# The last 800 steps of a hand-ordered attention and MLP kernel in another order, some copies and masks on another engine

## The chip, the cores and the metric

The kernel runs on one NeuronCore of a Trainium2 chip. It has five engines that each work through their own list of instructions in order: TensorE (PE; its weight loads are shown as PEld), VectorE (DVE), ScalarE (ACT), GpSimd (POOL) and SyncE (SP, here only an issuer of DMAs). The metric is the device time of one execution in microseconds: 209.23 us, the median of three runs (209.04 to 209.62).

## The reference

Windowed attention with four sink keys, then an MLP with a squared relu, on four batches of 768 tokens with eight heads of 64:

```python
scores = scale * np.matmul(q, k.transpose(0, 1, 3, 2))
keep = is_sink | in_window          # key < 4, or 0 <= query - key < 128
a = softmax(np.where(keep, scores, -1e9))
x = np.matmul(a, v)                 # heads side by side: 3072 x 512
h = x @ w_in                        # 512 x 2048
r = np.maximum(h, 0.0)
out = (r * r) @ w_out               # 2048 x 512
```

## The kernel before

Each batch is six blocks of 128 tokens, taken as three pairs s = 0, 1, 2. For a batch, queries and keys are brought to a transposed layout `qkT`: batches 0 and 1 by TensorE (`transpose`, L503, then `unload` through L192 or L194), batches 2 and 3 by DMA transpositions that SP issues (`turn`, L460) from bf16 copies `qn`, which POOL's DMAs load (L402). For each pair and two head pairs, TensorE makes scores (`ps`, L609), ScalarE exponentials (`expm`, L630), and the window's triangles are masked, on DVE (L642 or, for a batch's first pair, L639) or on POOL in two instructions (L218). TensorE multiplies by the values (`po`, L678), DVE normalizes (L694, L695) into `xn_sb`. That is transposed to `xT`, by TensorE (L727) or, in batches 2 and 3, by SP (L709).

Layer 1 (L762, L892) works in PSUM tiles `pm`. From batch 1 on it uses a scheme with seven products in place of eight: sums `wi` of weights and `xs` of tokens stand as operands, copies of partial results `t` (L192 on ACT, L194 on DVE) are added by a custom DVE instruction (L942) or go through a relu (L967, L969), and the result is squared into `gT_sb` (L915 on ACT, L917 on DVE). For one pair of blocks alone the tokens are first spread by a copy `xd<-xT` on ACT (L192). Layer 2 (L1239) does the same per pair of blocks, called tile (b, u): four sums of `gT_sb` on DVE (L1213, into `sg` or in place), seven products into `py`, evacuations to `osb` (L192, L194, L1253), and a store by SP (L1282, 512 KB). The very last tile (3, 2) has a form of its own (L1058, L1100, L1125, L1141, L1148) whose stores are four of 128 KB (L1168, L1183, L1186).

Nothing plans at run time or build time. The 992 steps are created in a fixed order and numbered by it; a table of words, `ORDER`, says in which order they are issued. A word is the step's number, a letter for the engine (d, a, g; none where the step has its first choice), and after a + the PSUM pool of a tile, 0 or 1 for the first or second of the pools that it may take. `Plan.run` (L94) walks the table: it takes a room for each tile that a step needs, first free first, issues the step, and gives rooms back after their last reader. So the table sets each engine's order, and with it which earlier reader a new tile waits for.

```python
for word in words:
    word, *chosen = word.split("+")
    n = int(word.rstrip("pdag"))
    o = self.ops[n]
    o.engine = names[word[-1]] if word[-1] in names else next(iter(o.engines))
    for s in o.takes:
        if len(s.pools) > 1:
            s.pool = s.pools[int(chosen.pop(0))]
        s.room = free[s.pool].pop(0)
    o.run(o.engine)
```

PSUM has two pools, `att` and `den`, of two rooms each; a room holds one tile of two banks. The SBUF pool `qr` of five rooms holds the `qn` tiles, so that batch 3's loads wait for batch 2's turns.

Of the kernel before, what the change touches and what calls it, by code (L numbers as in the profile page):

```python
# [22 lines left out]
63a 68+0 75+1 88d 69 70 76+1 22 71+0 77 23 72 73 78 24 94a 79+1 90+0 93d 92a 95+1 80 91d 81 96a 74 100+0 82 101+0 25  # L23
26 102 83+1 97d 66 84d 27 104 85 110+1 111+0 103g 86d 152+1 112 28 113d 105d 98+0 99 153 106+0 108 114 115d 154a 116+1
118 29 160+1 109 161 162a 107 30 119 117 120+0 31 155d 163a 122 121d 123d 32 168+0 156+1 331 33 172+0 157 169 164+1
170a 165 34 35 158d 173 166a 124+1 125a 127+0 36 159d 176+1 129a 177 126d 174a 140+1 133+1 37 128d 171d 142 136 180+1
181 282+0 38 178d 167d 137d 132+0 141+1 182a 130+0 39 283 40 144 143d 41 134 42 43 332 284 285 131 145d 146+0 175a 147
135g 278 179a 286 138+1 139 287 288 148+0 150 334 151d 44 149a 279 183d 289 184+1 290 185 193+0 280 281 200+0 201 291
194 45 204+1 196+0 202 46 203 205 198a 186 197 207a 293 206 187+0 199a 216+0+0 47 48 195a 217 49 188d 234+1+0 50 235
190+0 219 208+0 87 292 237 209 295 191 218 297+0 189 220 51 336 52 212 53 210a 294 211 255+0 252+1 254 299 298 256 54  # L30
253a 257 444 223+0+1 333 238d 445 192a 226 304 213 224 221+0 312 222 300 241+1+0 301 214+0 296 244 215 302 225 446
303d 242 306 260+0+0 236 462 263 307 314 337 316+0 245d 243d 315 227 308 313 447 318 319 464 246+0 261 247 239+0 448
240 320 321 228+0 475 322d 317 229 258+0 335 259 325 449 450 310 326 230+0 451 231 452 232 248+0 233 249a 327 250 251a
323 309 305 343+1 359+1 339 338 344 467 340 345 341 360 463 329 311 453 324 328 346 465 347 361 362 363 267+1+1 348
349 350 364 268 342 365d 270 351d 366 367 375+0 352 376 377 354 368 454 355 468 356d 370 369a 357 455 391+0 456 379
264 457 262 466 458 265+0 271 393 353 459 378 269 371 392 395 358a 266 372 272+0 373 381 380 382 474 374a 397 394 273
274+0 383d 276 277 396 275a 384 469 407 386 485+0+0 388d 718 472 387 470 460 486 398 410 461 408 389 412+1 488 471
478+1+0 409 399 473 385 479 400 487 330 413 688 402 414 428+0 404 401 403 405 430 416 429 418 432 406a 489 530+0 481
415 390 417 431 419 532 689 526 411 490+0 434 420 433 435 528 421 423 491 436 437 707 482 527 422a 533 424 480 534 690
708 476+0 477 425 439 440 441 691 535 442 531 483+1 426 529 484 443a 536 494+0+0 537 438a 497 692 427 495 568+0 545  # L40
539 540 570 564 566 492 693 694 695 542 498d 501+0+0 502 565 696 541 493 571 504 697 706 538 572 698 543 569 709
517+0+1 518 546 699 573 544 547 520 700 575 503d 510+0+0 701 574 549+0 496d 583 711 576 567 577 584 578 521d 513 505
579 585 551 581 506+0 552 580 507 514 511 586 512d 553 519 713 588+0 499+0 710 500 554 702 703 555d 515+0 516 522+0
589 719 550 590 712 523 591 745+0+0 748 592 558 556 548 560 746 738+0+0 741 594d 557 593 587 595 559 562 739 561
722+0+0 747 596d 714 604+0 749d 725 597 606 599 605 600 726 601 608 607 715 508 509 723 602 524 716 525 717 656+1 657
598 720+0 658 609 620 721 659 610 622 640+0 750+0 724 611 642 612 621 641 751 613 742 603a 660 662 740 615 644 623 646
614 727+0 616 704 661 617 663 563 643 645 618 647 619 672+0 664 667 665 648 651 649 728 582 674 668 673 669 650 676
670 743+0 652 666a 675 744 653 624+1 678 671a 677 654 626 679 625 729+1+0 680 730 628 770 681 655 630 683 774+0 771
732 684 627 775 685 686 629 772 776 754+0+1 682a 755 731 631 777 687 733 773 632 734+0 735 778 635 779 757 705 761+1+0
633 637 636 781 752 758 780d 634 762 638 756 639a 736 793+0 783 789 764 790 784 759+0 737 791 785 795 760 763 782 765  # L50
794 827 828 800 832+1 766+0 786 787 767 848+0 788 850d 829 833 808 796 834 835 830 849 797 768 836 838d 810 851 753
798 837 852 812+1 792 839 853 799 854 855 856 769 801 802 804 840d 859 803 841 857 831 814 843 815 858 842a 866 844
861 805d 816 845 811 809 806 860 817 868+0 813 862 864 846 819 865 818 863 869 870 884+1 867 871 821 872 885 874 823
886d 873 875 822 847 876 916+0 824 887 888 917 889 932 825 877 878 879 890 934 820 918 880 919 920 900+1 807 902 881d
882 933 891 921 883a 901 892 904 936+0 922d 938 906 903 923 905 893 924d 895 896 907 925 894a 897 939 935 908d 927 898
928 926a 940 929 937 826 911 909 899a 913 910 930 941 931 912 942 914 943 946 915 970 955+1 944 945 957 951 974+0 948
953 971 947 952 958 975 949 959d 956 972 960 950 961 973 977+0 962 976 978 964 954 966 979d 965 963 980 968 981 982
985 967d 969 983 984 989 986 988 987
"""
DUMMIES = {  # L60
    57: 9, 62: 14, 95: 7, 83: 3, 991: 29,
# [1348 lines left out]
```

## Time and profile before

| what | us |
|---|---|
| median of three runs | 209.23 |
| profiled execution, its own time | 209.26 |
| its span, first to last instruction | 207.6 |
| busy: PE, PEld, DVE, ACT, POOL | 199.6, 176.2, 174.7, 133.9, 96.2 |
| first changed steps, about | 44 |
| last matmul ends, about | 204.2 |
| last store issued | 204.57 |

A time in the profile is counted from the span's start. Times and lines of the profile are of the kernel before; in the changed kernel every line of the functions has a number higher by four, since the table has four rows more (L218 is L222 there, L1213 is L1217). A busy TensorE may still be waiting a little, since the end of each matmul is modelled and overlaps the start of the next; the idle time of the weight loads shows shorter waits. "issue" as a releaser means that the profile shows nothing that was waited for.

### The profile page before, as it was taken

Reading aid. Unit: us, or ns where it says so; the run is one execution under the profiler, and the core shown is the slowest. Engines: PE = TensorE matmul, PEld = TensorE weight load, DVE = VectorE, ACT = ScalarE, POOL = GpSimd, SP = SyncE. Lnnn points to the kernel's source line nnn. Section 1 sums busy time; section 2 is a strip of 40 time slices with the busy share of each in tenths; the row PEclk is TensorE's granted clock in tenths of the full one; section 3 lists DMA queues with packets and bytes.
Section 4 is the critical chain, followed back from the end, with each engine's and each line's share of the span. In section 5 each row is a group of like instructions: output and inputs, shape, how many; then the busy total and the mean of one; then the engine's idle time right before and its main releaser. Section 6 shows DMA issues by size and latency. Waiting matters only on the chain.

```text
span 207.6 us, 6021 instructions
## 1 busy us (share of the span) xinstructions
PE 199.6 (96%) x2500; PEld 176.2 (85%) x2502; DVE 174.7 (84%) x342; ACT 133.9 (64%) x208; POOL 96.2 (46%) x137
## 2 busy tenths in 40 slices
PE   7969999999899999999999999999999999999993
PEld 7458997579878899889878988998889999999893
DVE  4387657498899998999998778999989998998853
ACT  2769458729998168898888458989871452584010
POOL 7799275699499927999333529000280000000000
PEclk9999999999999999999999999999999999999999
DMA  5999999999999999999999996901023220200205
GB/s 157 220 218 200 186 185 212 180 156 175 159 75 126 147 129 225 117 182 155 123 142 235 103 135 194 115 3 25 12 42 129 53 94 10 104 0 0 104 0 202
DMA packets 96042, 26.10 MB, mean 126 GB/s; under 512 B 86800, under 2 KB 93456, under 8 KB 96016
## 3 DMA queue, kind: packets, MB, share of 16 engines
q0 software_dynamic: 69248, 12.59, 86.5%
q1 hardware_dynamic: 25568, 12.49, 27.2%
q10 hardware_dynamic: 1200, 0.66, 1.1%
q8 instruction: 19, 0.31, 0.6%
q14 instruction: 7, 0.06, 0.1%
HBM read 27.30 MB, written 6.29 MB: 162 GB/s over the span
## 4 chain that ended last, share of the span: by engine, by line
PE 80%; DVE 6%; ACT 6%; DMA 4%; issue 2%; POOL 0%; ACTq 0%; POOLq 0%; DVEq 0%
PE py L1239 28%; PE pm L892 25%; PE pm L762 9%; PE po L678 6%; PE ps L609 4%; DMA v<-in_v_dram 4%; PE py L990 3%; ACT expm L630 2%; PE py L1100 2%; PE pt L503 1%; DVE r L942 1%; ACT gT_sb L915 1%; PE px L727 1%; DVE xn_sb L695 1%; ACT qkT L192 1%
## 5 line engine op out<-in xcount | busy, mean ns | idle before, releaser
L630 ACT ACTIVATE expm<-ps 128x1024 bf16<-128x1024 f32 (+1 forms) x48 | 43.8, 951 | 9.6 <-PE ps L609 7.6
L218 POOL TENSOR_SCALAR_AFFINE_SELECT expm<-expm 128x512 bf16<-128x512 bf16 x34 | 24.0, 740 | 42.2 <-DVE xn_sb L695 19.5
L942 DVE CUSTOM_DVE_ANT_0 r<-pm,t 128x512 bf16<-128x512 f32 x54 | 36.0, 684 | 1.6 <-PE pm L892 1.2
L1239 PEld LDWEIGHTS <-gT_sb 128*128 128x128 bf16 x320 | 30.4, 98 | 4.4 <-issue 0.6
L892 PEld LDWEIGHTS <-w_in_sb 128*128 128x128 bf16 x384 | 32.4, 114 | 1.7 <-issue 1.5
L192 ACT ACTIVATE t<-pm 128x512 f32<-128x512 f32 x42 | 24.7, 600 | 13.4 <-PE pm L892 12.7
L892 PEld LDWEIGHTS <-wi 128*128 128x128 bf16 x288 | 24.7, 114 | 0.8 <-issue 0.7
L1239 PEld LDWEIGHTS <-sg 128*128 128x128 bf16 x240 | 22.5, 98 | 3.1 <-DVE sg L1213 0.3
L192 ACT ACTIVATE osb<-py 128x256 f32<-128x256 f32 (+1 forms) x36 | 14.1, 397 | 15.7 <-PE py L1239 15.0
L762 PE MATMUL pm<-xT,w_in_sb 128*128 128x256 bf16 x192 | 22.5, 273 | 0.1
L892 PE MATMUL pm<-xs,wi 128*128 128x256 bf16 (+1 forms) x192 | 21.6, 246 | 0.0
L892 PE MATMUL pm<-xs,w_in_sb 128*128 128x256 bf16 (+1 forms) x192 | 21.5, 246 | 0.0
L762 PEld LDWEIGHTS <-w_in_sb 128*128 128x128 bf16 x192 | 20.5, 114 | 0.8 <-issue 0.5
L1239 PE MATMUL py<-wt,gT_sb 128*128 128x256 bf16 x160 | 20.7, 273 | 0.2
L1239 PE MATMUL py<-wt,sg 128*128 128x256 bf16 x160 | 20.8, 273 | 0.0
L1239 PE MATMUL py<-w_out_sb,gT_sb 128*128 128x256 bf16 x160 | 20.4, 273 | 0.0
L915 ACT ACTIVATE gT_sb<-r 128x1024 bf16<-128x1024 bf16 x17 | 18.0, 1056 | 1.8 <-DVE r L942 1.6
L678 PE MATMUL po<-v,expm 128*128 128x65 bf16 x352 | 17.9, 193 | 1.1 <-DMA v<-in_v_dram 1.1
L678 PEld LDWEIGHTS <-expm 128*128 128x128 bf16 x352 | 16.8, 97 | 2.3 <-issue 1.3
L695 DVE TENSOR_TENSOR xn_sb<-po,rc 128x512 bf16<-128x512 f32 (+1 forms) x28 | 17.2, 615 | 1.0
L1253 DVE TENSOR_TENSOR osb<-py,osb 128x256 f32<-128x256 f32 x30 | 12.1, 416 | 4.7 <-PE py L1239 4.6
L609 PE MATMUL ps<-qkT 64*128 64x128 bf16 (+1 forms) x256 | 14.5, 238 | 1.1 <-ACT expm L630 0.6
(107 smaller groups left out, 377.8 us busy)
## 6 DMA issues: line engine op xcount, KB each, us to landing
out_dram<-osb SPq DMA_DIRECT2D x11, 512.0 KB, 3.0
v<-in_v_dram POOLq DMA_DIRECT2D x24, 128.0 KB, 7.0
qn<-in_k_dram POOLq DMA_DIRECT2D x20, 128.0 KB, 6.6
qn<-in_q_dram POOLq DMA_DIRECT2D x20, 128.0 KB, 6.3
w_in_sb<-in_moe_w_in_dram POOLq DMA_DIRECT2D x4, 512.0 KB, 9.2
w_out_sb<-in_moe_w_out_dram POOLq DMA_DIRECT2D x4, 512.0 KB, 10.5
qr<-in_k_dram SPq DMA_DIRECT2D x4, 256.0 KB, 6.9
qr<-in_q_dram ACTq DMA_DIRECT2D x2, 256.0 KB, 4.2
```

The costliest lines, as they stand in the source:

```text
L192: return nc.scalar.activation(out=dst, in_=src, func=AF.Copy)
L218: nc.gpsimd.affine_select(out=e_tile, in_=e_tile, compare_op=ALU.is_ge, fill=fill, base=i - 1, pattern=[[0, n], [1 if i else -1, 128]], ch ...
L609: nc.tensor.matmul(ps[:, h2, o:o + w], lhsT=qkT_sb[r, m, 1, c, :], rhs=qkT_sb[r, m, 0, qb:qb + w // 128, :], start=(i == 0 and not biased) ...
L630: nc.scalar.activation(out=x[:, :, o:512], in_=bank_t["s", b, s, m][:, :, o:512], func=AF.Exp, scale=scale)
L678: touch(("po", b, s, m0), e, nc.tensor.matmul(pv[:, i, h2, :], lhsT=lhsT, rhs=rhs, start=(n_ == 0), stop=(n_ == len(mms) - 1)), j)
L695: touch(("po", b, s, m0), e, nc.vector.tensor_tensor(out=xn_sb[:, 2 * s:2 * s + 2, 128 * (m0 + j0):128 * (m0 + j0 + nj)].rearrange("p i (j ...
L762: nc.tensor.matmul(pm[:, i, :], lhsT=w_in_sb[:, fb // 4, kb, fb % 4:512:4], rhs=xT[:, c0 // 256:(c0 + cw) // 256, kb, :], start=(kb == 0), ...
L892: touch(tag, e, nc.tensor.matmul(y[:, bk, i, :], lhsT=weights(name, f0 + i, a), rhs=rhs[:, a, :], start=fresh and i == 0 and a == 0, stop= ...
L915: nc.scalar.activation(out=d, in_=x, func=AF.Square)
L942: touch(tag, e, nc.vector._custom_dve(TENSOR_ADD_SAT, out=d.rearrange("p n c -> p (n c)"), in0=T["y"][:, 1].rearrange("p n c -> p (n c)"), ...
L1239: touch((b, u), e, nc.tensor.matmul(region(name), lhsT=x[:, i, :], rhs=w_[:, i, :], start=first and i == 0, stop=i == HB - 1, skip_group_c ...
L1253: ins = nc.vector.tensor_tensor(out=d, in0=region(of), in1=d, op=ALU.add)
```

## The change

Only the table changes. Its first 188 words issue the same steps as before (they carry more letters). From the 189th on, near 44 us, where batch 1's first scores are prepared, the remaining 800 or so steps stand in another order up to the end. Of these, 75 name another engine: on balance four masks more go to POOL (six go there, two come back), and copies, relus and squares are exchanged between DVE and ACT in both directions. Twenty PSUM tiles or so take the other pool. The steps themselves, their matmuls, their sizes and all DMAs are the same.

```diff
 ORDER = """
-990 1 0 2 7 8 9 10 11 12 13 14 15 16 17 18 56d 60a 55d 991+0 3 19 57+0 61d 20 5 6 4 62+1 65 59a 67+0 58a 21 64d 89d
...
-985 967d 969 983 984 989 986 988 987
+990d 1d 0d 2d 7 8a 9 10a 11 12 13 14 15 16 17 18 56d 60a 55d 991+0 3g 19g 57+0 61d 20g 5g 6g 4g 62+1 65g 59a 67+0 58a
...
+965 963d 982 968d 967a 985 969 983d 984d 989 986d 988 987d
 """
```

Three places show how rows move. The first is TensorE at batch 1's first scores (`ps` are scores, `pt` transposes of queries and keys from `qn`). Before, the second score step follows the first directly:

```order
L609 LDWEIGHTS qkT_180
L609 MATMUL ps<-qkT_180 128x256
L609 LDWEIGHTS qkT_180
L609 MATMUL ps<-qkT_180 128x128
L609 LDWEIGHTS qkT_180
L609 MATMUL ps<-qkT_180 128x128
```

In the changed kernel eight transposes, each with its weight load, stand between the first step and the second (one of the eight pairs is shown):

```order
L613 LDWEIGHTS qkT_180
L613 MATMUL ps<-qkT_180 128x128
L507 LDWEIGHTS qn
L507 MATMUL pt<-ident,qn 128x128
...
L613 LDWEIGHTS qkT_180
L613 MATMUL ps<-qkT_180 128x128
```

They are the transposes of the batch's third head pair, which stood ahead of the score steps before.

The second place is SP's queue in batches 2 and 3 (`qkT_179` and `qkT_180` are the layouts of batch 2 and batch 3, `xT_184` is batch 2's token layout). Before:

```order
L1282 DMA out_dram<-osb 128x1024
L460 DMA_TRANSPOSE qkT_179<-qn 128x4x128 x8
L460 DMA_TRANSPOSE qkT_180<-qn 128x4x128 x2
L709 DMA_TRANSPOSE xT_184<-xn_sb 128x4x128 x2
L460 DMA_TRANSPOSE qkT_180<-qn 128x4x128 x2
L1282 DMA out_dram<-osb 128x2x512
L460 DMA_TRANSPOSE qkT_180<-qn 128x4x128 x6
L709 DMA_TRANSPOSE xT_184<-xn_sb 128x4x128 x3
```

Now:

```order
L464 DMA_TRANSPOSE qkT_179<-qn 128x4x128 x7
L1286 DMA out_dram<-osb 128x1024
L464 DMA_TRANSPOSE qkT_179<-qn 128x4x128 x4
L464 DMA_TRANSPOSE qkT_180<-qn 128x4x128 x4
L713 DMA_TRANSPOSE xT_184<-xn_sb 128x4x128 x2
L464 DMA_TRANSPOSE qkT_180<-qn 128x4x128 x6
```

Four turns of batch 3, not two, stand ahead of the first two transpositions of `xT_184`.

The third place is DVE at the sums of layer 2's last two tiles (L1213 is tile (3,1), L1058 tile (3,2); `sg` holds sums). Before:

```order
L1058 TENSOR_TENSOR sg<-gT_sb 128x1024
L1253 TENSOR_TENSOR osb<-py,osb 128x256 x2
L1213 TENSOR_TENSOR sg<-gT_sb 128x1024
L1213 TENSOR_TENSOR sg<-sg,gT_sb 128x1024
L1058 TENSOR_TENSOR gT_sb<-gT_sb 128x8x128
L1213 TENSOR_TENSOR gT_sb<-gT_sb 128x8x128
```

Now:

```order
L1257 TENSOR_TENSOR osb<-py,osb 128x256
L1062 TENSOR_TENSOR sg<-gT_sb 128x1024
L1217 TENSOR_TENSOR sg<-gT_sb 128x1024
L1217 TENSOR_TENSOR gT_sb<-gT_sb 128x8x128
L1217 TENSOR_TENSOR sg<-sg,gT_sb 128x1024
```

One of the two evacuations ahead of the sums went to a later place, and tile (3,1)'s sum in place now precedes its second sum into `sg`.

More of the change, by code (lines that the diff above doesn't have):

```diff
@@ new lines @@
+153 106+0 108 114a 115d 154a 116+1 118 29g 160+1 109d 161 162a 107d 30g 119d 117d 120+0 31g 155d 163a 122 121d 123d
+32g 168+0 156+1 331d 33g 172+0 157 169 164+1 170a 165 34g 35g 158d 173 166a 124+1 125a 127+0 36g 159d 176+1 129a 177
+126d 174a 140+1 133+1 37g 128d 171d 142a 136a 180+1 181 282+0 38g 178d 167d 137d 132+0 141+1 182a 130+0 39g 283 40g
+144a 143d 41g 134a 42g 43g 332d 284 285 131a 145d 146+0 175a 147d 135g 278d 179a 286 138+1 139d 287 288 148+0 150 334d
+151d 44g 149a 279d 183d 289 280d 200+0 196+1 87g 333d 290a 184+1 293d 202a 45g 46g 198d 295d 291a 193+0 185a 194a 201
@@ new lines @@
+203d 47g 197 187+1 199a 48g 216+0+1 217a 335d 188d 204+1 206a 205 234+0+0 207d 235a 49g 195d 294d 219a 190+0 208+0
+212g 50g 209 237a 51g 218d 52g 191a 53g 297+0 220d 252+0 189d 299a 253a 54g 221+1 300 210d 254d 255+0 238g 211a 222d
+223+0+1 186d 301a 256d 444g 192d 213a 226a 302 298 224a 445g 257a 241+0+1 312d 303a 281d 214+0 314d 306d 304 244a 292
+215a 446g 308 447g 260+0+1 296d 245g 242a 261a 258+0 236g 259a 307 225d 462 243g 239+0 227d 310d 448g 263a 309a 230+0
+313d 305d 449g 240d 311 231a 228+1 229d 316+0 450g 246+0 232 465 264g 451g 262g 464 452g 318d 319 247d 248+1 453g 250
@@ new lines @@
+317 320d 315d 249a 251d 321 468 233a 339d 323 454g 336d 343+1 455g 322a 359+1 344 340d 345a 347 456g 360 325d 326 361a
+338d 341d 342d 328a 324d 337d 349a 363 327 346d 469 329d 348 362d 365a 267+1+1 457g 268a 350 364 351d 366 270a 352d
+367a 353d 391+0 354 356a 355 393a 375+0 368d 357d 370 372a 371 265+0 458g 358d 459g 377a 376 369a 379 463 467 373d
+271g 266d 472 378d 381a 269g 272+0 273d 392 274+0 374a 460g 380 275a 382 394d 330 276 395 277d 383a 384d 485+0+0 386
+473 396 407a 461g 387 385d 474g 408d 486a 688g 397a 412+1 689g 488a 398 414a 399a 413 388d 389d 478+1+0 409d 471 470
@@ L59 @@
+940a 941 909d 910a 930d 912 898d 935d 937 913a 943 914d 931a 942d 955+1 915d 946 945d 899a 970d 951d 947 952d 953d
+957a 944d 971d 954d 974+1 956 948d 958 949d 972d 959a 975 960 977+1 979d 962 973d 950 961d 976a 978 964d 981 966 980d
+965 963d 982 968d 967a 985 969 983d 984d 989 986d 988 987d
 """
```

57 lines of the change are left out of this document (22 added, 35 removed).

## The prediction

> **What bounds the kernel now.** I read the page first, its busy times, then the table of stretches from the first changed steps to the last matmul (columns: stretch, length, busy time and count of PE, PEld, DVE, ACT and POOL, granted clock, DMA share, GB/s).
>
> ```profile
> PE 199.6 (96%) x2500; PEld 176.2 (85%) x2502; DVE 174.7 (84%) x342; ACT 133.9 (64%) x208; POOL 96.2 (46%) x137
> 80.00:100.00 20.00, 19.85 (x289) 18.31 (x287) 19.82 (x39) 18.35 (x29) 19.26 (x27) 1.00 1.69 151
> sum 160.20, PE 159.28 PEld 143.67 DVE 147.24 ACT 106.83 POOL 65.94; mean PE 19.91 PEld 17.96 DVE 18.40 ACT 13.35 POOL 8.24
> ```
>
> TensorE is busy in 159.28 of the 160.2 us from 44.0 to 204.2, at a granted clock of 1.00, and VectorE in 147.24. The changed steps issue the same matmuls, so a new order can only take away waits of TensorE, or make new ones. A busy PE hides waits shorter than its pipeline, so I went to the waits of the weight loads in the same stretch (us in total, times, longest), and to the places where they lie.
>
> ```profile
> PEld L609 <- issue: 3.8, 16, 0.7
> PEld L892 <- issue: 2.2, 12, 0.3
> PEld L1239 <- DVE gT_sb L1213: 0.4, 1, 0.4
> PEld L1239 <- DVE sg L1213: 0.3, 1, 0.3
> PEld L1239 <- DVE osb L194: 0.2, 1, 0.2
> ```
>
> The 16 pieces at L609 stand where scores begin after wider matmuls, some 0.2 us each; the new order has 15 such places in place of 16, so 0.2 us at most goes there. The 0.7 among them and the three DVE rows are true waits: 0.7 + 0.4 + 0.3 + 0.2 = 1.6 us. That is all that an order can be seen to win on this engine; what it can lose has no such bound.
>
> **The change part by part.** The sum is made against the profiled execution, 209.26 us, of which 207.6 are span and 1.7 lie around it; the median shown is 209.23.
>
> *First scores of batch 1.* Two score steps follow each other; the second waits for PSUM that the exponentials of the first give back.
>
> ```profile
> 52.61 0.40 PE L609 MATMUL ps<-qkT 64*128 64x128 bf16 x6 [0.58 <-ACT expm L630]
> 52.62 0.17 PEld L609 LDWEIGHTS <-qkT 64*128 64x128 bf16 x5 [0.70 <-issue]
> 54.72 0.61 PE L503 MATMUL pt<-ident,qn 128*128 128x128 bf16 x8
> 55.16 1.04 PE L1239 MATMUL py<-w_out_sb,gT_sb 128*128 128x256 bf16 x8
> ```
>
> Now eight transposes of L503 stand between the two. Eight of them last 55.16 - 54.72 = 0.44 us, and they were work of the time before 51.3 anyway. So 0.44 of the 0.70 is filled. Bounds: 0 (the relu at L778 gives back the other bank, and ends as late) and -0.7. I take -0.45, since the exponential itself does not move.
>
> *The two waits for sums of layer 2.* The products that waited (steps 794 and 958 of the table) come later on TensorE now.
>
> ```profile
> 152.64 1.01 DVE L1213 TENSOR_TENSOR sg<-gT_sb 128x1024 bf16<-128x1024 bf16 x1 [0.83 <-ACT gT_sb L915]
> 153.69 1.07 DVE L1213 TENSOR_TENSOR gT_sb<-gT_sb 128x1024 bf16<-128x1024 bf16 x1
> 154.82 0.44 PEld L1239 LDWEIGHTS <-gT_sb 128*128 128x128 bf16 x5 [0.41 <-DVE gT_sb L1213]
> 192.77 0.69 DVE L1213 TENSOR_TENSOR sg<-sg,gT_sb 128x1024 bf16<-128x1024 bf16 x1
> 193.51 0.77 PEld L1239 LDWEIGHTS <-sg 128*128 128x128 bf16 x8 [0.31 <-DVE sg L1213]
> ```
>
> Between 784 and 794 TensorE had a values step and one product (759, 785), now two values steps and one product (759, 766, 796). Between 947 and 958 there was nothing, now two products (974, 956). One step lasts some 0.8 us and a product 0.87 (two stand at 200.54 and 201.41, rows below), so each has at least 0.8 us more cover against 0.41 and 0.31. On VectorE the sum for 958 has one sum more ahead of it (0.69) and one evacuation less; that for 794 comes one sum and one evacuation later, but the layer-1 product whose square starts these sums (636) stands some 1.4 us of matmuls earlier, and the square is on DVE itself now (0.70 by the L917 row below, in place of about 1.07, as the ACT copy of that size at 110.53 below). Bounds 0 and -0.72; I take -0.6. The 0.2 behind a copy I leave as it is.
>
> *The engines.* By the words of the table: six masks go from DVE to POOL and two back; of squares eight leave DVE and seven come (two of them of batch 0); of the copies of partial sums (`t`) nine leave and four come, of layer 1's relus one leaves and four come; of layer 2's evacuations six leave and twelve come; two smaller copies leave on balance.
>
> ```profile
> L642 DVE TENSOR_TENSOR expm<-expm,tri 128x1024 bf16<-128x1024 bf16 x15 | 10.4, 714 | 2.6 <-ACT expm L630 2.6
> L218 POOL TENSOR_SCALAR_AFFINE_SELECT expm<-expm 128x512 bf16<-128x512 bf16 x34 | 24.0, 740 | 42.2 <-DVE xn_sb L695 19.5 <-ACT expm L630 16.4 <-issue 6.3
> L917 DVE TENSOR_TENSOR gT_sb<-r 128x1024 bf16<-128x1024 bf16 x19 | 13.3, 701 | 0.4
> L194 DVE COPY t<-pm 128x512 f32<-128x512 f32 x12 | 8.2, 685 | 1.0 <-ACT expm L630 0.6 <-PE pm L892 0.4
> L194 DVE COPY osb<-py 128x256 f32<-128x256 f32 x7 | 2.9, 417 | 0.2 <-PE py L1239 0.2
> ```
>
> DVE: -4 x 0.714 - 1 x 0.70 - 2 x 0.685 + 6 x 0.417 - 2 x 0.417 = -3.3 us of 147. POOL: 4 masks of two instructions, 8 x 0.74 = +5.9 us of 66. ACT gains about 1 us of 107. None of these is a term by itself, since TensorE ends every stage; the cover is the order in front of each consumer. One place is thin: three of batch 1's masks that were on DVE now stand on POOL, behind the loads of batch 2, and the first values step of its second pair of blocks comes about 2 us earlier on TensorE. Counting POOL's queue, its mask ends just in time. Bounds 0 and one mask, 2 x 0.74 = 1.48; I take +0.2, nearer to no wait.
>
> POOL and DVE also slow each other: with POOL's masks running, the two sums at 152.64 and 153.69 took 1.01 and 1.07, the one at 192.77, with POOL idle, 0.69. [...]
>
> *The tail.* The three products ahead of the final two change places (the last two rows are of the table of DMA issues, with KB and us to landing).
>
> ```profile
> 200.54 1.04 PE L1239 MATMUL py<-w_out_sb,sg 128*128 128x256 bf16 x8
> 201.41 1.04 PE L1100 MATMUL py<-w_out_sb,sg 128*128 128x256 bf16 x8
> 202.18 0.37 SPq L1282 DMA_DIRECT2D out_dram<-osb  x1
> 202.28 1.04 PE L1100 MATMUL py<-wt,gT_sb 128*128 128x256 bf16 x8
> 202.48 0.42 DVE L1125 TENSOR_TENSOR u<-py,u 128x256 f32<-128x256 f32 x1 [0.33 <-PE py L1100]
> 203.36 0.69 DVE L1148 TENSOR_TENSOR osb<-py,u 128x512 f32<-128x512 f32 x1
> 204.57 0.35 SPq L1168 DMA_DIRECT2D out_dram<-osb  x1
> out_dram<-osb SPq DMA_DIRECT2D x11, 512.0 KB, 3.0
> out_dram<-osb SPq DMA_DIRECT2D x3, 128.0 KB, 1.9
> ```
>
> Tile (3,2)'s product at 201.41 moves two products forward, so the sum into `u` that waited for it need no longer wait; but L1148 needs the product at 202.28 as well, which ends at 203.15 as before, so the chain to the last store at 204.57 stays: 0. Tile (3,1)'s last product now ends at 202.3 instead of 201.4, and its 512 KB store issues at about 203.0 instead of 202.18. With 3.0 us to land, that is 206.0 to 206.4, against 204.57 + 0.35 + 1.9 (landing of the 128 KB stores) = 206.8 for the last small one. Bounds 0 and 0.8; nearer the first, +0.1.
>
> Sum: 209.26 - 0.45 - 0.6 + 0.2 + 0.1 - 0.1 (half of the one score switch less) = 208.4.
>
> **The rivals.**
>
> *All true waits go, nothing new comes:* 209.26 - 1.6 = 207.7. For it: DVE has 3.3 us less to do, and three of the four waits name it. Against: in the stretch from 80 to 100 DVE is busy in 19.82 of 20 us, so short waits are likely to come anew.
>
> *Waits come back elsewhere:* as many steps as before stand less than a microsecond behind what they need, so the 1 us won is lost in small pieces: 209.2. Against it only that the known waits are the long ones.
>
> *The slow side: a transposed block of batch 2 comes late.* SP works in order, and a transposition there waits for its load.
>
> ```profile
> 95.31 1.83 POOL L402 DMA_DIRECT2D qn<-in_q_dram  x2
> 102.57 2.50 SPq L709 DMA_TRANSPOSE xT<-xn_sb  x2
> 110.53 1.07 ACT L192 ACTIVATE xd<-xT 128x1024 bf16<-128x1024 bf16 x1
> 115.18 0.61 PE L892 MATMUL pm<-xd,w_in_sb 128*128 128x128 bf16 x8
> DMA to landing us min/median/max: 2.4/6.2/12.7
> DMA to landing us min/median/max: 2.4/4.2/7.3
> ```
>
> (The last two are of tiles `qn` and `xT`.) Before, two transpositions of batch 3 stood ahead of the `xT` pair at 102.57, now four, and the fourth needs the load at 95.31. Batch 3's loads wait for the turns of batch 2, and those for their loads, between which three more masks now stand on POOL: 3 x 1.48 = 4.4 us, of which POOL's idle time there takes back about half, an estimate. So the load starts 2.2 later, at 97.5, is issued in 0.9, lands 6.2 later at 104.6, its turn lasts 1.25 like each of the pair at 102.57, and the `xT` pair ends 2.5 after that, at 108.4 against 105.1. With the median landing of 4.2 it is there at 112.6, the spread copy (1.07) done at 113.7, and TensorE wants it near 114.4 (115.18 less what is won before): nothing lost. With the longest, 7.3, it is done at 116.8: 2.4 us lost, 208.4 + 2.4 = 210.8. It decides as soon as landing takes over 4.9 us. Before, the same pair had 3.6 us to spare (111.6 to 115.18), now 0.7.
>
> *The slow side: POOL's masks.* Each of the 8 added POOL instructions can hold DVE by 1.07 - 0.69 = 0.38 us, 3.0 in all, against the 2.9 that the masks save there. If a third of that meets a full DVE queue, 1.0 us; and a mask that ends 0.2 late at four of its consumers makes it 1.8. With the first term won, 209.26 - 0.45 + 1.8 = 210.6. It decides where DVE has no idle time, as from 80 to 100. Against: 34 such instructions run before, and the waits of PEld name DVE three times only.
>
> **How the numbers follow.** Forecast (208.4, by its own bounds 207.9 to 209.2) 0.45; all waits gone (207.7) 0.15; nothing won (209.2) 0.15; late block (210.8) 0.14; masks (210.6) 0.11. A measurement of this kernel tells about 0.3%, 0.63 us, from no change, so faster is below 208.6. The forecast's own case is split by that: 0.28 faster, 0.17 the same. Faster 0.28 + 0.15 = 0.43; same 0.17 + 0.15 = 0.32; slower 0.14 + 0.11 = 0.25. The range, 207.6 to 210.7, runs from the case of all waits gone to between the two slow ones, so that it leaves out the worse half of the late block and little more.
>
> **What would show it.** In the changed kernel's profile: the wait at the second score step near 52 at 0.3 or less; no wait of PEld for an L1217 sum over 0.2 near 155 and 193; PE's busy share from 44 on as now; the chain from the last `ya` matmul to the last store as long as before, and a 512 KB store issued near its end; POOL's L222 at 42 instructions. I am wrong on the slow side if PE shows a wait over 1 us near 114 with the spread copy `xd` ending there, or if DVE's two-input sums average over 0.8 us; wrong on the fast side if TensorE's many waits of 0.2 and 0.3 us "for issue" at L892 were waits for data after all and go.

## The result, and the profile after

The changed kernel takes 224.12 us (median), the kernel before 209.28 us beside it: 1.070 times as long, with an interval of 1.064 to 1.075. The forecast was 208.4 us, its range 207.6 to 210.7. Runs more than 1.5% above the fastest of their kernel are left out of the ratios and intervals here and below, while medians in us are of all runs. In the profiled execution (223.71 us) the span is 221.7 us, 14.1 more than before. TensorE does the same work; the difference is waiting, and some 1.7 us of a lower granted clock. The page's busy times, and the head of its chain of work that ended last (before: PE 80%, DVE 6%, ACT 6%, DMA 4%):

```profile
PE 202.6 (91%) x2502; PEld 177.0 (80%) x2502; DVE 178.0 (80%) x339; ACT 135.5 (61%) x207; POOL 105.2 (47%) x145
...
PE 66%; DVE 11%; DMA 9%; ACT 4%; issue 4%; POOL 3%; POOLq 1%; SPq 0%; DVEq 0%; ACTq 0%
```

The table of stretches shows where (columns as in the prediction: length, busy time and count of PE, PEld, DVE, ACT, POOL, granted clock, DMA share, GB/s):

```profile
60.00:80.00 20.00, 18.77 (x245) 16.23 (x244) 17.95 (x34) 11.52 (x20) 19.69 (x24) 1.00 1.41 118
80.00:100.00 20.00, 17.81 (x221) 15.92 (x216) 17.19 (x28) 15.34 (x24) 12.66 (x18) 0.91 1.66 149
100.00:120.00 20.00, 18.17 (x241) 14.91 (x240) 18.45 (x33) 16.98 (x28) 13.61 (x18) 1.00 1.95 135
120.00:140.00 20.00, 17.17 (x274) 15.03 (x271) 15.49 (x33) 9.96 (x13) 9.21 (x15) 1.00 1.39 143
140.00:160.00 20.00, 20.00 (x261) 18.27 (x260) 18.03 (x34) 17.41 (x28) 1.22 (x2) 1.00 0.14 42
160.00:180.00 20.00, 19.21 (x268) 17.93 (x266) 18.77 (x38) 11.98 (x20) 5.48 (x6) 1.00 0.21 55
```

Before, PE was busy in 19.85 to 20.00 of each 20 us from 60 on. Now 5 of the 6 stretches have gaps, and the one from 80 to 100 also a granted clock of 0.91 in place of 1.00. VectorE isn't fuller (17.19 in place of 19.82 from 80 to 100). What PE waited for (total, times, longest):

```profile
PE py L1243 <- DVE osb L1257: 2.4, 3, 1.0
PE pm L896 <- DVE r L946: 2.0, 1, 2.0
PE pm L896 <- DMA xT<-xn_sb: 2.0, 1, 2.0
PE po L682 <- DVE expm L646: 1.2, 1, 1.2
PE pm L896 <- DVE osb L198: 1.1, 1, 1.1
PE po L682 <- POOL expm L222: 1.1, 2, 0.8
PE pt L507 <- DMA qn<-in_q_dram: 1.0, 2, 0.7
```

So there isn't one wait but ten places, of 0.4 to 2.2 us. The list below is worked out from the matmuls of the trace: what a matmul starts later than the usual pace behind the one before it (a little more than the idle time in the rows above).

| near us | lost, us | TensorE's step, and what it waited for |
|---|---|---|
| 56 | 0.86 + 0.43 | transposes 252: loads of `qn` |
| 62 | 1.25 | product 304: evacuation 306 of the same PSUM bank |
| 67 | 0.42 | values 239: a mask on POOL |
| 83 | 2.20, and about 1.7 by the clock behind it | layer 1, 371: an addition on DVE, behind a square of 2.87 us |
| 111 | 0.77 | product 541: evacuation 538 |
| 118 | 1.38 | values 522: mask 519 on DVE |
| 134 | 2.19 | layer 1, 656: a block that SP transposes |
| 138 | 0.96 | product 560: evacuation 557 |
| 166 | 0.96 | values 766: mask 765 on POOL |
| 192 | 1.23 | layer 1, 900: PSUM that evacuation 824 gives back |

That is 14.35 us; the spans differ by 14.1.

### The profile page after: what moved, and what is told of

Same layout as the page of the kernel before. It is cut to its first block, busy times and chain, and to the rows that moved or that the text cites. A ratio compares the mean times of both kernels' runs of the same rounds, so it can differ in the third digit from the quotient of the medians.

```text
span 221.7 us, 6032 instructions
## 1 busy us (share of the span) xinstructions
PE 202.6 (91%) x2502; PEld 177.0 (80%) x2502; DVE 178.0 (80%) x339; ACT 135.5 (61%) x207; POOL 105.2 (47%) x145
## 4 chain that ended last, share of the span: by engine, by line
PE 66%; DVE 11%; DMA 9%; ACT 4%; issue 4%; POOL 3%; POOLq 1%; SPq 0%; DVEq 0%; ACTq 0%
PE pm L896 21%; PE py L1243 20%; PE pm L766 8%; PE po L682 6%; DMA v<-in_v_dram 4%; DMA xT<-xn_sb 3%; PE py L994 3%; ACT expm L634 3%; PE ps L613 3%; POOL expm L222 2%; DMA qn<-in_q_dram 2%; PE py L1104 2%; DVE sg L1217 2%; DVE gT_sb L921 1%; DVE expm L646 1%
## 5 line engine op out<-in xcount | busy, mean ns | idle before, releaser
L222 POOL TENSOR_SCALAR_AFFINE_SELECT expm<-expm 128x512 bf16<-128x512 bf16 x42 | 30.5, 760 | 38.9 <-ACT expm L634 32.6
L196 ACT ACTIVATE t<-pm 128x512 f32<-128x512 f32 x47 | 27.2, 603 | 22.5 <-PE pm L896 17.3
L196 ACT ACTIVATE osb<-py 128x256 f32<-128x256 f32 (+1 forms) x30 | 12.2, 405 | 20.5 <-PE py L1243 18.1
L919 ACT ACTIVATE gT_sb<-r 128x1024 bf16<-128x1024 bf16 x20 | 21.1, 1058 | 3.7 <-DVE r L946 2.0
L766 PE MATMUL pm<-xT,w_in_sb 128*128 128x256 bf16 x192 | 22.5, 273 | 0.1
L682 PE MATMUL po<-v,expm 128*128 128x65 bf16 x352 | 19.0, 196 | 3.5 <-DVE expm L646 1.2
L682 PEld LDWEIGHTS <-expm 128*128 128x128 bf16 x352 | 17.5, 100 | 5.5 <-DVE expm L646 1.7
L896 PE MATMUL pm<-xT,w_in_sb 128*128 128x256 bf16 x96 | 13.6, 279 | 3.1 <-DMA xT<-xn_sb 2.0
```

What stands on the lines that cost most here:

```text
L196: return nc.scalar.activation(out=dst, in_=src, func=AF.Copy)
L222: nc.gpsimd.affine_select(out=e_tile, in_=e_tile, compare_op=ALU.is_ge, fill=fill, base=i - 1, pattern=[[0, n], [1 if i else -1, 128]], ch ...
L682: touch(("po", b, s, m0), e, nc.tensor.matmul(pv[:, i, h2, :], lhsT=lhsT, rhs=rhs, start=(n_ == 0), stop=(n_ == len(mms) - 1)), j)
L766: nc.tensor.matmul(pm[:, i, :], lhsT=w_in_sb[:, fb // 4, kb, fb % 4:512:4], rhs=xT[:, c0 // 256:(c0 + cw) // 256, kb, :], start=(kb == 0), ...
L896: touch(tag, e, nc.tensor.matmul(y[:, bk, i, :], lhsT=weights(name, f0 + i, a), rhs=rhs[:, a, :], start=fresh and i == 0 and a == 0, stop= ...
L919: nc.scalar.activation(out=d, in_=x, func=AF.Square)
```

## The experiments

The theories as they stood: the loss is **in the order** (steps at a wrong place in a queue) or **in the engines** (75 steps moved, masks to POOL above all); and each wait **is made where it stands**, or is **lateness handed on** from an earlier one. Ratios go against the kernel before on the same chip, with 95% intervals; a ratio less 1, times 209.3, is given as "us over". Words in the diffs are those of `ORDER`.

### Order and engines apart

```diff
 e1: each word of the changed table, with before's engine letter
-... 198d ... 238g ... 303a ...
+... 198a ... 238d ... 303d ...
 e2: each word of before's table, with the changed engine letter
-... 198a ... 238d ... 303d ...
+... 198d ... 238g ... 303a ...
```

> The changed kernel's order with every step back on the engine it had before (the 75 engine changes undone, pools and order as changed). If the order makes the loss (loads, masks and transpositions issued at other places of POOL's and SP's queues), it stays near the changed kernel: 219 to 225 us, with TensorE again waiting for a load near 56, and for the layer-1 sum beside four POOL masks near 83. If the engine changes make it (masks on POOL, evacuations on a fuller DVE), it falls to 209 to 213.

> The kernel before with the 75 engine changes and its own order and pools. If the order makes the loss: 208.5 to 212. If the engine changes make it: 218 or more. The sum of this run's loss and that of the run with the order alone, against 14.8 us, shows whether the two add or one needs the other.

Measured: e1 1.0836 (1.0793 to 1.0879), 17.5 us over; e2 1.0781 (1.0746 to 1.0817), 16.3 us over. Both halves alone cost more than the whole (14.6). They don't add: an order fits one set of engines. By the same list of matmuls, e1 has six of the ten places (those of 62, 83, 111, 138, 166 and 192, with 0.56 to 1.51 us, 5.8 in all), which so come with the order; the loads (56) and the block (134) aren't late in it, so the changed engine letters bring those. Its other waits, some fifteen of 0.4 to 1.1 us, are its own. In e2, with the old order, PE's largest group of waits is for evacuations, those that ACT copied and that now stand in DVE's queue:

```profile
PE py L1239 <- DVE osb L194: 4.3, 2, 2.9
```

So "order or engines" was the wrong question. The new engines give 3 us back in the new order and cost 16 in the old one.

### Where it is made: the tables cut

At a few places the two tables have done nearly the same steps, so that one can be followed by the other.

```diff
 e9:  -changed table                 +its first 404 words (to 90 us), then the rest as in before
 e10: -before                        +its first 404 words (to 84 us), then the rest as changed
 e11: -before                        +its first 773 words (to 150 us), then the rest as changed
 e12: -changed table                 +its first 223 words (to 53 us), then the rest as in before
```

> The first 404 words of the changed table (to about 90 us, with the stalls near 56, 62, 67 and 83), then every other step in the order and on the engine of before; at this word the two tables differ in three steps only. If each stall is made where it stands: 209.3 plus what TensorE is behind at 92 us in the changed kernel (6.1, of which some 1.7 are a lower clock) = 213.5 to 215.5. If lateness handed on from there makes the later stalls (batch 2's and 3's loads are late by then): 218 or more. If the old order takes the lateness up: under 212.

> The reverse: the first 404 words of before (to about 84 us), then the order and engines of the changed table. If each stall is made where it stands: 224.1 - 6.1 = 218 (217 to 219), with the stalls near 111, 118, 134, 138, 166 and 192 about as they were. If the later stalls come from the early lateness: 209 to 213.

> The first 773 words of before (to about 150 us; the tables differ there in one step), then the changed table. If stalls are made where they stand: 209.3 + 0.96 (masks near 166) + 1.23 (evacuation near 192) = 211.5. If these too are lateness handed on: 209 to 209.8.

> The first 223 words of the changed table (to about 53 us, where TensorE stood 0.4 to 0.9 us ahead of the kernel before), then before. If that gain keeps: 208.4 to 208.9. If it is given back at the next wait: 209.0 to 209.6. If the old order behind it doesn't fit what was done first: over 210.5.

Measured: e9 1.0310 (1.0271 to 1.0348), 6.5 over. e11 1.0114 (1.0088 to 1.0139), 2.4 over. e12 1.0026 (1.0009 to 1.0043), 0.5 over. e10's four runs lie between 216.4 and 224.0 us, too far apart for an interval (the next part but one shows what varies). The stretches of e9 and of the changed kernel, from 92 us to the end of the matmuls and a little beyond (the second stretch of 128 us is the changed kernel's):

```profile
92.00:212.00 120.00, 119.26 (x1500) 107.74 (x1497) 109.40 (x209) 75.90 (x124) 32.25 (x40) 1.00 0.72 93
```

```profile
92.00:220.00 128.00, 119.21 (x1490) 106.84 (x1487) 109.12 (x209) 77.68 (x122) 33.84 (x44) 1.00 0.70 85
```

In e9 the late start (loads and all) costs nothing further: some 1500 matmuls take 120 us, in the changed kernel about 126 (the last ends near 217.8). And e11, which is in time up to 150 us, has the last two waits of the table at full size:

```profile
PE pm L892 <- DVE osb L194: 1.1, 1, 1.1
PE po L678 <- POOL expm L218: 0.8, 1, 0.8
```

So waits far apart are made where they stand: 6.5 us before 92, 2.4 after 150, and what is left, about 6, between. That the middle needs nothing from before 92 us was e10's question. Its lowest run is still 7 us over, so much of the rest comes without the early part; the other three are 11 to 14 over, so the size of the middle isn't settled by it.

### The first stretch: late loads, and a run of masks

```diff
 e3: the building of the window masks and the sink products behind the loads
-... 200+0 196+1 87g 333d ... 208+0 212g 50g 209 237a 51g 218d 52g 191a ...
+... 200+0 196+1 333d ... 208+0 50g 87g 209 237a 51g 218d 52g 212g 191a ...
 e14: one load between two masks
-458g 358d 459g 377a ... 271g 266d ... 269g
+458g 358d 377a ... 271g 459g 266d ... 269g
```

> The changed kernel with two POOL steps moved back behind batch 1's last loads of queries and keys: the building of the window masks (87) behind load 50 and the sink products (212) behind load 52, their places before. If late loads start the loss and it grows from them: the wait for qn near 56 (0.86 + 0.43) and the one for an evacuation near 62 (1.25) go, 224.1 - 2.5 = 221.6, and less if the later stalls follow from them (as low as 216). If POOL's masks make it on their own: 222.5 to 225, with the stalls at 83, 118 and 134 as they are.

> The changed kernel with one POOL step moved: the load 459 between the masks 271 and 269, as in the kernel before, so that POOL waits for the exponential of 271 instead of coming to it late and runs two mask instructions in a row, not four. [...]

*Loads.* e3: 1.0562 (1.0519 to 1.0605), 2.8 us less than the changed kernel. The changed kernel's timeline around 56 us (start, length, engine, line, operation):

```profile
51.84 1.76 POOL L375 DMA_DIRECT2D qn<-in_q_dram  x2
...
56.94 0.23 PE L507 MATMUL pt<-ident,qn 128*128 128x128 bf16 x1 [0.70 <-DMA qn<-in_q_dram]
57.43 0.45 PE L507 MATMUL pt<-ident,qn 128*128 128x128 bf16 x5 [0.26 <-DMA qn<-in_q_dram]
```

Before, the two loads were issued at 49.10. POOL builds masks (87) and sink products (212) ahead of them now, and the transposes 252 come no later. With the two steps behind the loads this wait is gone; the one at 62 stays at 1.25, so it isn't handed on from there. The 2.8 us are more than the 1.3 of this wait: in e3's profile the block at 134 is 0.83 late in place of 2.19 (and an evacuation 1.19 late at 127, which is new), and the clock stays at 1.00 behind the wait at 83, which is 1.7 us that the edit wasn't meant to win.

*Masks in a row.* At 83 the changed kernel shows a square of 2.87 us in place of 0.68, while POOL works off four mask instructions; TensorE stands for 2.04 us, and in the two stretches of 2 us behind it its granted clock is 0.65 and 0.50:

```profile
82.18 2.45 POOL L222 TENSOR_SCALAR_AFFINE_SELECT expm<-expm 128x512 bf16<-128x512 bf16 x4
82.32 2.87 DVE L921 TENSOR_TENSOR gT_sb<-r 128x1024 bf16<-128x1024 bf16 x1
85.84 0.60 PE L896 MATMUL pm<-xs,w_in_sb 128*128 128x256 bf16 x4 [2.04 <-DVE r L946]
```

```profile
84.00:86.00 2.00, 0.16 (x2) 0.16 (x2) 2.00 (x3) 0.72 (x2) 2.00 (x4) 1.00 2.09 147
86.00:88.00 2.00, 1.91 (x30) 1.61 (x29) 1.83 (x3) 1.48 (x2) 1.88 (x4) 0.65 1.64 170
88.00:90.00 2.00, 2.00 (x17) 1.56 (x16) 1.59 (x3) 0.27 (x1) 0.45 (x2) 0.50 2.33 155
```

By these two clocks (1 - 0.65) x 2 + (1 - 0.50) x 2 = 1.7 us go, an estimate, and so are the losses by the clock below. Four matmuls of 128x256 hold TensorE for 0.84 us from 87.80 on (the next begin at 88.64), and for 0.44 from 91.12 on (to 91.56), where the clock is 1.00 again. In e14, where POOL waits for the first mask's exponential and has a load before the second mask, the same square takes 1.00 us:

```profile
84.75 1.67 POOL L222 TENSOR_SCALAR_AFFINE_SELECT expm<-expm 128x512 bf16<-128x512 bf16 x2 [0.79 <-ACT expm L634]
84.92 1.00 DVE L921 TENSOR_TENSOR gT_sb<-r 128x1024 bf16<-128x1024 bf16 x1
```

Its stretch from 80 to 100 in the table of stretches:

```profile
80.00:100.00 20.00, 19.57 (x256) 17.55 (x254) 17.98 (x33) 17.19 (x27) 13.49 (x19) 1.00 1.77 155
```

PE is busy in 19.57 of the 20 us, at a granted clock of 1.00, in place of 17.81 at 0.91: the place is cured by one moved word. The whole kernel isn't: e14 measured 1.0755 (1.0668 to 1.0843). The profiled execution is the longest of its four (227.88 us; the others took 223.59 to 226.93 and have no profile). In it, what was won is lost again: the loads at 56 are 2.2 late, the store of the next part costs 4 us, and the clock was lower twice (0.95 from 44 to 80, 0.83 from 120 to 140), for some 5.1 us in all.

### The middle: masks against sums, a store behind turns

```diff
 e4: eight mask letters back
-238g 243g 245g 496g 503g 521g 519d 742d
+238d 243d 245d 496d 503d 521d 519g 742g
 e16: e14, and the store of tile (1,0) ahead of six turns on SP
-541 543d 713 567d ... 711 ... 708 ... 710 ... 714 ... 715 ... 544
+541 543d 544 713 567d ... 711 ... 708 ... 710 ... 714 ... 715
```

> The changed kernel with only the eight mask changes undone (238, 243, 245, 496, 503, 521 on DVE, 519 and 742 on POOL). If masks on POOL hold up POOL's loads and the values steps: the stalls at 67 (0.42), 118 (1.38), 134 (2.19) and 138 (0.96) go, 224.1 - 4.9 = 219.2. If the loss is in the order of POOL's other steps: 223 to 225.

> The kernel of e14 with one step moved on SP's queue: the store of tile (1,0), 544, ahead of six turns of batch 3, behind the evacuation that completes its data, as in the kernel before. If the late store holds the output buffer and so the evacuation 551 and the product 552: the wait of 4.1 near 128 falls under 0.6, the time to 221 to 223, and the runs lie closer (e14: 223.6 to 227.9). If 552 waits for another reason: 224 to 228 as before.

e4: 1.0474 (1.0406 to 1.0541), 4.7 us less than the changed kernel, the largest single part. That is near the 4.9 expected, but by another sum, so the match is luck. Of the four waits named, those at 67 and 134 are gone; those at 118 (1.04) and 138 (1.55) aren't, and the loads at 56 were 2.2 late in this execution. In their place the wait at 83 is 0.33 and the clock stays at 1.00 behind it, together 3.6 us. With fewer masks ahead, POOL waits there for the first of its four masks, and the square takes 1.01:

```profile
83.41 2.84 POOL L222 TENSOR_SCALAR_AFFINE_SELECT expm<-expm 128x512 bf16<-128x512 bf16 x4 [3.37 <-ACT expm L634]
83.58 1.01 DVE L921 TENSOR_TENSOR gT_sb<-r 128x1024 bf16<-128x1024 bf16 x1
```

e16: 1.0741 (1.0699 to 1.0784), no faster than e14, though the wait that it aims at was there. In e14 SP issues the store of tile (1,0) behind six turns that wait for batch 3's loads, at 125.09; its last evacuation (543) was done at 113.4. Until it has landed the output buffer isn't free, so DVE waits 4.54 us with an evacuation, and TensorE 3.92 for that (before, SP issued this store at 108.68, ahead of those turns):

```profile
116.50 8.50 SPq L464 DMA_TRANSPOSE qkT<-qn  x6
125.09 0.55 SPq L1286 DMA_DIRECT2D out_dram<-osb  x1
...
131.58 0.42 DVE L198 COPY osb<-py 128x256 f32<-128x256 f32 x1 [4.54 <-DMA out_dram<-osb]
...
132.06 1.86 PE L1243 MATMUL py<-wt,sg 128*128 128x256 bf16 x8 [3.92 <-DVE osb L198]
```

With the store early, that wait is gone in e16, and the four runs lie within 1.6 us (e14: 4.3). The same wait stood in the profiles of e6 (2.7), e10 (3.8) and e3 (1.0), and not in the changed kernel's. But the next transposed block is late, by 3.12 us:

```profile
135.52 1.01 PE L896 MATMUL pm<-xT,w_in_sb 128*128 128x256 bf16 x4 [3.12 <-DMA xT<-xn_sb]
```

Behind it the granted clock is 0.67, 0.50, 0.50 and 0.62 in the four stretches of 2 us from 134 to 142, another 3.4 us or so. So lateness is handed on here, among the turns, blocks and stores in SP's one queue. In the changed kernel's profiled execution the store landed just in time and the block was 2.0 late; in e14's it was the other way round.

### Product and evacuation in one bank

A PSUM tile of layer 2 has two banks, and the product 304 and the evacuation 306 work in one of them. Neither needs the other's data. Before, 304 was issued first; in the changed table 306 is, 304 waits 0.97 us for it, and it stands in DVE's queue behind a sum over weights and a sum:

```profile
61.39 1.22 DVE L1035 TENSOR_TENSOR wt<-w_out_sb,wt 128x2048 bf16<-128x2048 bf16 x1
62.53 0.69 DVE L1217 TENSOR_TENSOR sg<-sg,gT_sb 128x1024 bf16<-128x1024 bf16 x1
63.13 0.42 DVE L1257 TENSOR_TENSOR osb<-py,osb 128x256 f32<-128x256 f32 x1
...
63.60 0.60 PE L1243 MATMUL py<-w_out_sb,gT_sb 128*128 128x256 bf16 x4 [0.97 <-DVE osb L1257]
```

The same holds for 541 behind 538 and 560 behind 557.

```diff
 e5: evacuations earlier on DVE
-312d 303a 281d 214+0 314d 306d 304      564d 505g 493 502a 566d 538d
+312d 303a 306d 281d 214+0 314d 304      564d 538d 505g 493 502a 566d
-606a 620d 607d 724d 657 608 557d 560    820d 878a 887d 880 807 934d 825d 923 824d
+606a 557d 620d 607d 724d 657 608 560    820d 825d 824d 878a 887d 880 807 934d 923
 e13: products ahead of them on TensorE
-302 298 ... 306d 304                    540 712 492 568+0 ... 538d 542d 541
+298 304 302 ... 306d                    540 712 492 541 568+0 ... 538d 542d
-558d 656+1 ... 557d 560
+558d 560 656+1 ... 557d
```

> The changed kernel with five evacuations of layer 2 issued earlier on DVE, ahead of sums that stood before them (306 ahead of a weight sum and a sum, 538 ahead of one sum, 557 ahead of two steps that wait for a late transposition, 825 and 824 ahead of a sum and a layer-1 addition). If evacuations behind sums make four of the stalls: 0.8 of the 1.25 near 62, 0.7 of the 0.77 near 112, 0.96 near 138 and 1.2 near 192 go, 224.1 - 3.7 = 220.4. If these waits only show a DVE that is late anyway, another step is late in their place: 222.5 to 225.

> The changed kernel with three products of layer 2 moved on TensorE: 298 and 304 ahead of 302, 541 ahead of 568, 560 ahead of 656, so that each stands ahead of the evacuation (306, 538, 557) that reads the other half of its PSUM bank, as in the kernel before. DVE's own order is unchanged. If that order of product and evacuation makes the waits near 62, 112 and 138: 1.25 + 0.77 + 0.96 go, 224.1 - 3.0 = 221.1. If DVE is simply late there, the products or their neighbours wait as before: 223 to 225.

e5: 1.0600 (1.0554 to 1.0646), about 2 us less, half of what was expected; in place of the wait at 62 there are gaps of 0.49, 0.26, 0.55 and 0.49 at 304 and three steps behind it, and the wait for values 522 grew from 1.38 to 3.00. e13: 1.0693 (1.0631 to 1.0756), nothing. The waits at 62 and 112 went (0.44 is left at 62, none at 112), so the bank order makes them. At 138 product 560 still waits 0.68, now for the evacuation 558 behind which it was moved. But what was won came back: the wait for values 522 grew from 1.38 to 3.00 here too, since TensorE came earlier to values whose mask stands on DVE behind a sum that took 2.59 us beside POOL's masks:

```profile
117.56 2.59 DVE L1217 TENSOR_TENSOR sg<-sg,gT_sb 128x1024 bf16<-128x1024 bf16 x1
...
117.78 2.87 POOL L222 TENSOR_SCALAR_AFFINE_SELECT expm<-expm 128x512 bf16<-128x512 bf16 x4
...
121.25 0.23 PE L682 MATMUL po<-v,expm 128*128 128x65 bf16 x2 [2.84 <-DVE expm L646]
```

Behind this wait the granted clock is 0.85, 0.50 and 0.80 in the three stretches of 2 us from 120 to 126, another 1.7 us or so.

### Do the repairs add?

```diff
 e6:  two masks from POOL to DVE (269; 765, behind 764), one mask of DVE (519) ahead of 498 and 547
-269g ... 764a 780a 763g 765g ... 518a 503g 571 498d 547d ... 519d
+269d ... 764a 765d 780a 763g ... 518a 519d 503g 571 498d 547d
 e7:  e3 + e5 + e6
 e15: e3 + e4 + e13 + e14
 e17: e15, 544 as in e16, 765 as in e6, 825 and 824 as in e5
 e18: e15, 765, 825 and 824 so, and words 482 to 656 (97 to 129 us) in before's order
```

> The changed kernel with two POOL masks on DVE (269 near 83, 765 near 164: each was the second of two masks in a row on POOL, beside squares and sums of DVE) and one DVE mask (519) ahead of the mask and the sum before it. If masks in a row on POOL hold up DVE's two-input instructions: the stall of 2.20 near 83 goes with the lower clock behind it (about 1.7), the 0.96 near 166 and the 1.38 near 118 go, 224.1 - 6.2 = 217.9, and no square of DVE takes over 1.2 us near 83. If DVE has no room for two masks more: 222 to 225.

> The edits of the three runs e3, e5 and e6 together. If the stalls are of separate causes, the gains add: 1.3 + 3.7 + 6.2 = 11.2, 212.9, and 210.7 if the transposed block that is late near 134 (2.19) was late because of them. If each repair only hands the lateness on to another step, 216 or more.

> The changed kernel with the edits of e3, e4, e13 and e14 together (loads first, the eight masks back, product ahead of evacuation, a load between two masks). If the causes add: the measured 1.9 of e3 and 4.3 of e4, 3.0 for the banks and up to 1 for the masks near 83 give 224.1 - 10 = 214. If they only hand lateness on: 217 or more. What is left then should be the waits near 118 and 166 (masks), 134 (a transposed block) and 192 (an evacuation), 4 to 5 us.

> The kernel of e15 with the store moved as in e16, the mask 765 on DVE, and the evacuations 825 and 824 behind 820. If the waits near 166 (0.96) and 192 (1.23, of which e5 won 0.6) are made there, and the store costs the 0.47 seen at 552: 219.4 - 0.96 - 0.6 - 0.4 = 217.4. If they are handed on: 219 or more.

> The kernel of e15 with 765, 825 and 824 as in e17, and the words from 482 to 656 (about 97 to 129 us: batch 2's masks, layer 2 of batch 1, SP's turns of batch 3) in the order and on the engines of before. If the rest of the loss is made in that stretch: 217.8 less the 4.0 that TensorE fell behind there and the 0.9 just after = 213. If it is handed on from before 97 us or made after 129: 216 or more.

| run | ratio (interval) | us over | expected time, measured median |
|---|---|---|---|
| changed | 1.0698 (1.0642 to 1.0754) | 14.6 | |
| e6 | 1.0673 (1.0634 to 1.0712) | 14.1 | 217.9, 223.8 |
| e7 | 1.0584 (1.0542 to 1.0627) | 12.2 | 212.9, 221.6 |
| e15 | 1.0479 (1.0430 to 1.0528) | 10.0 | 214, 219.4 |
| e17 | 1.0433 (1.0360 to 1.0507) | 9.1 | 217.4, 217.8 |
| e18 | 1.0261 (1.0225 to 1.0296) | 5.5 | 213, 215.2 |

e6 missed. The waits at 118 and 166 shrank (to 0.68 and 0.30). But with 269 on DVE the square at 83 still took 1.71, and the mask on DVE made TensorE wait 1.90 at 87, so DVE had no room for it; and the late store costs 2.91 at 130. In e7 the 1.90 is there again, a product waits 1.43 at 119 and the block 1.23 at 135. Nor do the repairs add within the middle: e15 has the edits of e4 and three more, and is no faster than e4. Its profile says why. Up to 97 us it is all but cured (PE 51.54 busy of 53, the changed kernel 48.37), but from 97 on TensorE only comes earlier to the same masks and sums. In e18 that stretch has the old order, and the loss there is gone (first e15, then e18):

```profile
97.00:133.00 36.00, 32.17 (x469) 26.95 (x467) 31.10 (x59) 25.41 (x40) 25.38 (x32) 1.00 1.70 149
```

```profile
97.00:131.00 34.00, 33.67 (x493) 28.90 (x491) 30.53 (x59) 24.73 (x41) 21.66 (x29) 1.00 1.53 140
```

In e15 five DVE instructions in a row from 110.3 on take 1.11 to 1.12 us each in place of 0.68, with POOL's masks and loads beside them. That they set the pace there is read from the trace; no run took this alone away, since e18 changes the whole stretch. e17 against e15 shows the tail as expected: 766 waits no more (a gap of 0.31 at the next step), and 0.65 is left of the 1.23 at 192. By e18 9.1 of the 14.6 us are undone by named steps and one stretch. The 5.5 left lie in small waits: near 62 to 67 (0.73, 0.29, 0.39), 82 to 85 (0.33, 0.26, 0.27), 100 (0.44), 131 (1.11, for a turn), 160 and 185 (0.31, 0.65); these sum to 4.8, and 0.7 isn't accounted for (the kernel before has waits of 0.3 to 0.75 of its own, which the list doesn't take off).

### What the prediction counted as gains

```diff
 e8, from before
-204+1 196+0 202 46 203 205 198a ... 207a 293 206 ... 188d 234+1+0     952 958 975
+196+0 202 46 203 198a ... 293 ... 188d 204+1 205 206 207a 234+1+0     952 975 958
```

> The kernel before with only two of the rearrangements that the prediction counted as gains: the eight transposes of 204 and 205 between batch 1's two score steps, and the product 958 behind the product 975, so that its sum has 0.87 us more. By the prediction's sum: 209.26 - 0.45 - 0.31 = 208.5. If the time won is lost at the next tight place: 209.0 to 209.6. If any step out of its place costs as much as the engine changes alone did: over 211.

e8: 1.0015 (0.9994 to 1.0037): nothing is won. Its timeline, the middle row of waits at 72, and the last of the weight loads:

```profile
52.55 0.62 PE L609 MATMUL ps<-qkT 64*128 64x128 bf16 x12 [0.33 <-DVE r L778]
...
72.62 1.03 PE L1239 MATMUL py<-wt,gT_sb 128*128 128x256 bf16 x8 [0.42 <-DVE osb L1253]
...
194.69 0.77 PEld L1100 LDWEIGHTS <-gT_sb 128*128 128x128 bf16 x8 [0.92 <-DVE gT_sb L1058]
```

The second score step now waits for the relu of the other bank, 0.33; the time won is waited off at 72 for an evacuation; and the product that stands in 958's place waits for its own sum, 0.92 in place of 0.31.

## Why the prediction was wrong, step by step

**The step that failed** is in the part on the engines: "None of these is a term by itself, since TensorE ends every stage; the cover is the order in front of each consumer." The cover was counted at one thin place (values behind POOL's masks, +0.2) and taken as given at all others. The runs showed ten places where it wasn't there, 12.65 us of waits in place of the 0.3 that the sum has for all losses, and 1.7 us of a lower clock, which the sum doesn't have at all. A TensorE busy in 159.28 of 160.2 us was read as a bound that hides other engines' waits. It says that operands seldom came late, and nothing of how early they came. The prediction wrote that what an order can lose "has no such bound", and then bounded it by two mechanisms. Its signs for the slow side didn't show either: there is no wait near 114 with `xd`, and the sums of L1217 average 0.70 to 0.78 us (squares of L921 0.86, masks of L646 0.84).

**First scores, -0.45.** The wait shrank (0.75 to 0.41 in the changed kernel), and in e8 the bound that the prediction named, the relu at L778, ends what is left. But e12, which keeps the changed table up to there, is 0.5 us slower than before, and e8 no faster: the time is waited off at the next tight place. The rival "waits come back elsewhere" was right on this term.

**The two sums of layer 2, -0.6.** Both waits are gone in the changed kernel, as forecast. e8 shows for 958 that the wait comes from a queue of sums on DVE: the product that stands in its place waits.

**A late mask, +0.2.** The eight mask letters cost 4.7 us by e4. Of these, 3.6 are at 83 in e4's profile, where POOL has three masks less ahead of it. POOL's queue was counted up to the masks themselves, not to the loads behind them, nor to DVE's instructions beside them.

**Masks beside DVE, 0.38 per instruction.** That price came from two sums (1.01 and 1.07 beside masks, 0.69 without). No run shows one price for each instruction of POOL: beside masks the square took 0.32 us more in e14 (1.00) and 2.2 more in the changed kernel (2.87), and behind TensorE's wait of 2.2 there the lower clock took some 1.7 more: 3.9 us at one place, more than the 1.8 of the whole rival.

**The late block, a rival with a chance of 0.14.** The queue was the right one, SP's with batch 3's turns ahead of a block and its loads behind three more masks. The packet was another: not the pair near 108 but the block of 656 (2.0 late) or the store of tile (1,0) (3.9 in e14). That store had been moved behind six turns, which the order shows; the prediction looked on SP only for transpositions.

**Product and evacuation in one bank, 3.0 together.** Neither a term nor a rival; e13 took away 1.9 of it. The order shows it (306 ahead of 304), though no data pass between them.

**The tail, +0.1.** Right: the last store is issued 1.6 us after the last sixteen matmuls begin (216.74 to 218.32), before 1.4 (203.16 to 204.57); the 512 KB store is issued at 216.47, and the sum into `u` waits no more.

**The chances.** Each slow rival was one mechanism, priced at 1.8 and 2.4 us. They weren't alternatives: both came in kind, at other places than forecast and together with others, and waits as far apart as those before 92 and after 150 us add (e9, e11).

## What to carry to other kernels

That the bounding engine hardly waits says nothing of how much room its operands have, so a new order has to be followed to every consumer: where a queue of in-order work (SP's stores and turns, POOL's loads and masks, DVE's evacuations) changed ahead of one, 0.4 to 2.2 us were lost here, and such losses far apart in time add. Order and choice of engine belong together: each half of this change alone cost more than both. A repair must be judged over the whole stretch, since the time won at one step was often waited off at the next (e13, e16).

## What the runs showed of the hardware that was not expected

*A square beside four of POOL's masks took four times as long, or not.* In the changed kernel four masks ran in 2.45 us (0.7 each, a new one every 0.59) and the square that began beside the first took 2.87 in place of 0.68. In e14, where POOL had waited 0.79 us for the first mask's input, two masks took 1.67 and the square beside them 1.00. Four masks in a row alone don't make the long form: in e4, where POOL had waited 3.37 us for the first, four ran in 2.84 and the square took 1.01. The long form stood where POOL began its masks straight behind a load, without a wait (at 82.18 in the changed kernel, and at 117.78 in e13, where a sum took 2.59); in e3 the square took 2.86. That this decides it was not tested, and in the kernel before it was not enough: two masks begun at 81.28 without a wait took 1.69, and the square at 81.80 beside them 0.69.

*The clock can fall behind a wait of 2 us, or not.* Behind the wait of 2.04 us at 83 the granted clock was 0.65 and 0.50 for two stretches of 2 us. In e3 the same wait (2.03) at the same place left it at 1.00, and so did e6's wait of 2.91 near 130 (1.00 from 120 to 140). The stretches of e3:

```profile
84.00:86.00 2.00, 0.61 (x5) 0.38 (x5) 1.90 (x4) 1.25 (x3) 2.00 (x4) 1.00 2.49 143
86.00:88.00 2.00, 2.00 (x46) 1.99 (x47) 1.97 (x4) 1.17 (x2) 1.79 (x4) 1.00 1.97 162
88.00:90.00 2.00, 2.00 (x35) 1.98 (x32) 1.97 (x5) 1.82 (x3) 0.00 (x0) 1.00 1.92 192
```

What decides whether the clock falls isn't shown by these runs.
